# A hand-searched instruction order cut to the first half of weight conversion, and value-mean moves unchained, in a block-attention and gated-product kernel

## Chip, cores and metric

The kernel runs on one core of a Trainium2 chip. The metric is the device time of one execution in microseconds, as the median of several runs. PE is TensorE (matmuls), DVE is VectorE, ACT is ScalarE, POOL is GpSimd, and SP is SyncE, whose queue issues almost all transfers.

## The reference

```python
def attention(q, k, v):              # 4 sequences, 8 heads, 768 tokens, 64 wide
    k_sum = k.reshape(B, H, 24, 32, 64).max(axis=3)
    v_sum = v.reshape(B, H, 24, 32, 64).mean(axis=3)
    local = where(abs(pos_q - pos_k) < 16, q @ k.T / 8, -1e9)
    short = q @ k_sum.T / 8 + log(32)
    a = softmax(concat([local, short]))
    return a @ concat([v, v_sum])

def moe(x, w_a, w_b, w_out):         # x: 3072 x 512, hidden width 1536
    return ((x @ w_a) * (x @ w_b)) @ w_out
```

The output of the attention, with the heads laid side by side, is the x of the second part. All is float32.

## The kernel before

**Work and tiles.** The 3072 tokens are cut into tiles of 128, and these into ten chunks u = 0 to 9: three of two tiles for each of the first two sequences (u0 to u2, u3 to u5), two of three tiles for each of the last two. A chunk's attention makes scores (line 649), a softmax, transposed probabilities (line 786) and the product with the values (line 802). Its second part goes over twelve slices f = 0 to 11 of the hidden width. One *item* is a chunk and a slice: on PE the two products with w_a and w_b (line 1058, "hidden pair", 24 matmuls for chunks of two tiles), then ACT copies one (line 1090), DVE multiplies (line 1093), ACT rounds (line 1095), DVE subtracts to get the remainder (line 1098), and PE adds the product with w_out (line 1135, "down", 6 matmuls) one item later. Every operand is held as a high and a low half, so that one product takes three matmuls.

**Weights.** The 36 parts of the weights (a slice's a, b, o) are loaded by SP (line 373, tiles raw) and converted into the two halves by `convert(i)`: ACT (398) writes one word's value to a slot, DVE (401) writes a second word to a PSUM bank (c0 or c1), DVE (409) joins them, ACT (414) writes the high half, POOL (417) the low half. Parts from 18 on share the slots S0.0, S0.1, S1.0, S1.1. Chunks u0 and u1 run interleaved while this goes on. u2 (`FILL = 2`) is the "third attention": its score tiles use the banks c0 and c1, which the conversion uses too.

**The second sequence.** u3 opens it. `prep_keys(1)` loads its keys in four sets (tiles kin, and S for every other one), DVE transposes them (line 537) and takes block maxima. `prep_values(1)` loads the values, POOL sums them to block means in the tile vm, and eight moves on SP copy vm into the space S0 (`summed`), from which they are copied into the values' tiles vw. The room S0.2 and the keys in the list `PU` stand for the same space, used by the third attention. The values' tiles vw serve one score tile at a time: `bring(1)` loads them anew once the first tile's product has run.

**Order.** Every operation is given to `Work` with an engine, a rank, an assumed duration and the keys that it reads and writes; a write follows all earlier uses of its key. `emit` runs once, when the program is built, and writes the instructions out. Each engine keeps this order on the chip. For engines with a list in `ORDER`, the listed operations come exactly in that order:

```python
if fixed.get(e):
    return [o for o in ops if o.index == fixed[e][-1]]
return [o for o in ops if o.index not in listed]
```

When an engine's list is used up, the planner takes, of the operations that are ready by its assumed durations, the one with the lowest rank. Line numbers below are those of the kernel before; the changed kernel has them up to 13 lines earlier.

Of the kernel before, what the change touches and what calls it, by code (L numbers as in the profile page):

```python
# [21 lines left out]

ORDER = {
# [7 lines left out]
    ],  # L31
    "ACT": [
# [11 lines left out]
    ],  # L44
    "DVE": [
# [12 lines left out]
    ],  # L58
    "POOL": [
# [4 lines left out]
    ],  # L64
# [6 lines left out]
    ],  # L71
}

# [76 lines left out]
def attention_moe(  # L150
# [10 lines left out]
    nc = tc.nc  # L161
# [156 lines left out]
    work = Work({"POOL": 10.2, "DVE": 2.3, "ACT": 2.3, "PE": 3.0, "SP": 0.8})  # L318
# [4 lines left out]
    def act(rank, takes, reads, writes, fn):  # L323
        work.add("ACT", rank, takes, 0.16, reads, writes, fn)

    def dve(rank, takes, reads, writes, fn):
        work.add("DVE", rank, takes, 0.19, reads, writes, fn)
# [51 lines left out]
    def convert(i):  # L379

        rank = CONVERT + i / 12
        bk, (space, x) = f"c{i % 2}", ROOMS[i >= EARLY][i % len(ROOMS[i >= EARLY])]
        room = f"{space}.{x}"
        z = bank[bk].rearrange("p (m n) -> p m n", n=P)
        e = slot(space, x)[0].rearrange("p (m n) -> p m n", n=P)
        raw, hi, lo = f"raw{i}", f"hi{i}", f"lo{i}"

        def word(x):  # L390
            return raws[i].rearrange("p (m n t) -> p m n t", n=P, t=2)[:, :, :, x]

        def half(x):
            if i not in homes:
                homes[i] = wp.tile([P, 4, 2, P], F32R, tag=f"P{i}", name=f"w{i}")
            return homes[i][:, :, x, :]

        act(CHAIN, 0.57, [raw], [room], lambda: nc.scalar.activation(  # L398
            e, word(1).bitcast(F32), AF.Prelu, scale=2.0**-112, alpha=-(2.0**32)
        ))  # L400
        dve(rank, 0.6, [raw], [bk], lambda: nc.vector.tensor_scalar(
            out=z.bitcast(I32), in0=word(0).bitcast(U32), scalar1=2.0**-29, scalar2=7.0,
            op0=ALU.mult, op1=ALU.min,
        ))
        near = i in ON_DVE
        t, key = (z, bk) if near else (e, room)
        dve(
            rank, 0.6, [room, bk], [raw, key],
            lambda: nc.vector.scalar_tensor_tensor(
                out=t.bitcast(I32), in0=e.bitcast(I32), scalar=3, in1=z.bitcast(I32),  # L410
                op0=ALU.logical_shift_left, op1=ALU.bitwise_or,
            ),
        )
        act(rank - 0.5, 0.52, [key, raw], [hi], lambda: nc.scalar.copy(out=half(0), in_=t))  # L414
        (dve if near else pool)(
            rank, 0.6 if near else 1.24, [hi, key], [lo],
            lambda eng=nc.vector if near else nc.gpsimd: eng.tensor_tensor(  # L417
                out=half(1), in0=t, in1=half(0).bitcast(F32), op=ALU.subtract
            ),
        )  # L420
# [99 lines left out]
    def prep_keys(b):  # L520
        rank = LATER + 2 * b - 0.5
        if b == 1:
            work.add("-", 0, 0, 0, (), ["S1.2", "S1.3"], lambda: None)
        for c in range(NP):
            i = c % 2 if b == 1 else 0
            kw = kins[i]
# [37 lines left out]
    def prep_values(b):  # L564
# [7 lines left out]
        def add(n, out, i0, i1, writes):  # L572
# [2 lines left out]
                lambda: nc.gpsimd.tensor_tensor(out=out, in0=i0, in1=i1, op=ALU.add),  # L575
            )

        for hg in range(2):
            vv = v[b, 4 * hg : 4 * hg + 4].rearrange("h (n t) d -> (h n) t d", t=BLK)
            y, pk = vm[: 4 * NS, hg], f"vm{hg}"  # L580
            for i in range(BLK // T):
# [14 lines left out]
                        add(n, x[:, :n], x[:, :n], x[:, n : 2 * n], keys)  # L596
                        add(n, y, y, x[:, :n], keys + [pk])
            pool(
                rank, 0.3, (), [pk],
                lambda y=y: nc.gpsimd.tensor_scalar(  # L600
                    out=y, in0=y, scalar1=1.0 / BLK, scalar2=None, op0=ALU.mult
                ),
            )
            for h in range(4):
                load(
                    99, 6.0, 20, [pk], [VS[4 * hg + h]] + (["S0.2"] + PU if b == 1 else []),
                    summed(b)[:, 4 * hg + h], y[h * NS : (h + 1) * NS],
                )

# [14 lines left out]
    def scores(u, t, qT, qk, s, sk, banks, lead=None, way="AA"):  # L624
# [65 lines left out]
        for h in range(2):  # L690
# [18 lines left out]
            else:  # L709
                for c in range(NP):  # L710
                    more = {"accum_out": sums[:, c : c + 1]} if way[h] == "A" else {}
                    act(
                        rank, 0.44 if more else 0.32, [f"{mk}m{h}", xk[h]],
                        ([f"{mk}l{h}{c}"] if more else []) + ([ek[c]] if masked else []),
                        lambda h=h, c=c, more=more: nc.scalar.activation(  # L715
                            y[h][:, c, :], x[h][:, c, :], AF.Exp, bias=m[:, 0, h, c : c + 1],
                            scale=1.0, **more,
                        ),
                    )
            if way[h] != "A":  # L720
# [16 lines left out]
                lambda r=r, sums=sums: nc.vector.reciprocal(out=r, in_=sums),  # L737
            )
            pool(
                rank, 1.05, lk, ek if masked else [sk[h]],  # L740
                lambda h=h, r=r: nc.gpsimd.tensor_tensor(  # L741
                    out=y[h], in0=y[h], in1=r[:, :, None].broadcast_to([P, NP, COLS]),
                    op=ALU.mult,
# [102 lines left out]
    def first_attention():  # L846
# [31 lines left out]
        for n in range(4):  # L878
# [7 lines left out]
            )  # L886
            if MEANS[n] == "D":
                dve(
                    FIRST, 1.1, key, [f"vr{n}"],
                    lambda x=x, hg=hg, a=a: nc.vector.tensor_reduce(  # L890
                        out=rows[:, hg, a, :], in_=x.rearrange("p (t d) -> p d t", d=D),
                        axis=AX.X, op=ALU.add,
# [2 lines left out]
            else:  # L895
                m = 512
# [355 lines left out]
```

## Time and profile before

| what | value |
| --- | --- |
| median of three runs | 683.91 us (683.86 to 684.71) |
| profiled execution, its own time | 683.99 us |
| its span in the trace | 682.2 us, 13881 instructions |
| PE busy | 648.0 us (95%) |
| DVE busy | 403.5 us (59%) |
| ACT busy | 247.8 us (36%) |
| POOL busy | 156.1 us (23%) |

The busy times are sums over the whole span, and the engines are busy at different times: POOL, DVE and ACT do most of the conversion in the first 120 us, PE alone carries the rest. A share of the span therefore says little on one stretch; the rows further down are read by stretch.

### The profile page before, as it was taken

What the parts mean: (1) busy time and instruction counts of PE and PEld (TensorE: products, weight loads), DVE (VectorE), ACT (ScalarE), POOL (GpSimd) and SP (SyncE); (2) the same over time, 40 slices, a digit from 0 to 9 for tenths busy, and PEclk for the clock granted to TensorE, in tenths of its full rate; (3) what the DMA queues carried; (4) which work ended last, traced back from release to release, by engine and by line L of the source; (5) the groups of instructions that cost most, each with busy time, mean ns of one, the idle gap of its engine ahead of it and who ended that gap; (6) DMA issues with size and microseconds to landing.
All of it is one profiled execution on the core that took longest, in us unless ns stands there. A gap on an engine that the chain in (4) does not pass through costs nothing.

```text
span 682.2 us, 13881 instructions
## 1 busy us (share of the span) xinstructions
PE 648.0 (95%) x5384; PEld 607.4 (89%) x5384; DVE 403.5 (59%) x905; ACT 247.8 (36%) x748; POOL 156.1 (23%) x236
## 2 busy tenths in 40 slices
PE   5699999999955999999999999999999999999997
PEld 4488999899945999999999999999999999999996
DVE  4887779655566776945767777476767451121112
ACT  4798576321332333313433431243333421121111
POOL 6686264312533334301111010011111100000000
PEclk9699999999985999999999999999999999999999
DMA  9999950086235223432311213132211200010001
GB/s 210 261 310 235 313 176 1 2 163 142 71 93 102 61 62 65 106 56 52 76 38 38 68 38 60 33 84 39 40 24 25 69 1 1 1 46 1 1 1 46
DMA packets 153897, 54.76 MB, mean 80 GB/s; under 512 B 133976, under 2 KB 146520, under 8 KB 153832
## 3 DMA queue, kind: packets, MB, share of 16 engines
q1 hardware_dynamic: 153688, 53.75, 33.2%
q8 instruction: 42, 0.69, 0.4%
q14 instruction: 23, 0.19, 0.1%
q10 hardware_dynamic: 144, 0.13, 0.1%
HBM read 47.12 MB, written 6.29 MB: 78 GB/s over the span
## 4 chain that ended last, share of the span: by engine, by line
PE 85%; SPq 7%; DMA 3%; DVE 3%; ACT 1%; issue 1%; POOL 0%
PE h L1058 53%; PE o L1135 26%; SPq L335 6%; PE o L802 3%; PE c L649 3%; DMA raw<-in_moe_w_a_dram 2%; SPq L373 1%; DMA space<-in_v_dram 1%; DVE pt L786 1%; PE c L802 0%; DMA vw<-S 0%; DVE qT L1010 0%; PE c L1058 0%; DMA S<-vm 0%; ACT S L398 0%
## 5 line engine op out<-in xcount | busy, mean ns | idle before, releaser
L1058 PE MATMUL h<-x,w 128*128 128x256 f32 (+1 forms) x2488 | 397.8, 296 | 1.1 <-ACT x L821 0.7
L1058 PEld LDWEIGHTS h<-x,w 128*128 128x128 f32 x2488 | 356.9, 192 | 6.1 <-ACT x L821 0.9
L1058 PE MATMUL h<-late,w 128*128 128x256 f32 (+1 forms) x380 | 115.3, 303 | 0.1
L1135 PE MATMUL o<-w,gh 128*128 128x512 f32 x426 | 107.3, 383 | 0.0
L786 DVE STREAM_TRANSPOSE pt<-s 32x256 f32<-32x256 f32 x228 | 99.3, 436 | 11.7 <-POOL s L741 7.6
L741 POOL TENSOR_TENSOR s<-s,nml 128x480 f32<-128x480 f32 x44 | 43.4, 987 | 221.1 <-DVE nml L737 190.6
L1121 DVE TENSOR_TENSOR h<-h,g 128x384 f32<-128x384 f32 x47 | 26.6, 567 | 106.5 <-PE h L1058 106.3
L1135 PEld LDWEIGHTS o<-w,gh 128*128 128x128 f32 x426 | 76.3, 189 | 9.7 <-issue 1.4
L715 ACT ACTIVATE s<-s,nml 128x120 f32<-128x120 f32 x160 | 61.3, 385 | 42.6 <-DVE nml L686 42.5
L1123 ACT CAST gh<-h 128x384 fp32r<-128x384 f32 x47 | 22.5, 478 | 149.0 <-DVE h L1121 146.2
L1058 PEld LDWEIGHTS h<-late,w 128*128 128x128 f32 x380 | 73.3, 193 | 1.5 <-DVE late L825 0.4
L1093 DVE TENSOR_TENSOR h<-h,g 128x256 f32<-128x256 f32 x72 | 31.0, 431 | 67.9 <-ACT g L1090 67.4
L1090 ACT COPY g<-h 128x256 f32<-128x256 f32 x72 | 26.9, 373 | 116.3 <-PE h L1058 116.3
L1135 PE MATMUL o<-w,gl 128*128 128x512 f32 x213 | 59.7, 380 | 0.0
L1135 PE MATMUL o<-w,x 128*128 128x512 f32 x225 | 55.4, 382 | 0.4 <-ACT x L1095 0.3
L1135 PEld LDWEIGHTS o<-w,x 128*128 128x128 f32 x225 | 40.5, 189 | 6.7 <-ACT x L1095 1.3
L1135 PEld LDWEIGHTS o<-w,gl 128*128 128x128 f32 x213 | 40.1, 189 | 5.8 <-issue 0.2
L575 POOL TENSOR_TENSOR S<-S 96x256 f32<-96x256 f32 (+3 forms) x58 | 33.0, 570 | 46.0 <-DMA S<-in_v_dram 43.1
L1118 ACT COPY g<-h 128x384 f32<-128x384 f32 x48 | 23.0, 479 | 40.6 <-PE h L1058 40.1
L417 POOL TENSOR_TENSOR w<-S,w 128x512 fp32r<-128x512 f32 x24 | 30.5, 1284 | 30.2 <-ACT w L414 21.4
L1126 DVE TENSOR_TENSOR gl<-h,gh 128x384 fp32r<-128x384 f32 x47 | 26.2, 556 | 17.3 <-ACT gh L1123 16.8
L678 DVE SCALAR_TENSOR_TENSOR s<-c,mask 128x480 f32<-128x480 f32 x40 | 26.0, 653 | 14.4 <-PE c L649 14.2
(132 smaller groups left out, 572.2 us busy)
## 6 DMA issues: line engine op xcount, KB each, us to landing
raw<-in_moe_w_out_dram SPq DMA_DIRECT2D x12, 512.0 KB
raw<-in_moe_w_a_dram SPq DMA_DIRECT2D x12, 512.0 KB
raw<-in_moe_w_b_dram SPq DMA_DIRECT2D x12, 512.0 KB
out_dram<-S SPq DMA_DIRECT2D x23, 256.0 KB
S<-in_v_dram SPq DMA_DIRECT2D x24, 192.0 KB
kin<-in_k_dram SPq DMA_DIRECT2D x38, 100.0 KB
vw<-in_v_dram SPq DMA_DIRECT2D x17, 192.0 KB
qin<-in_q_dram SPq DMA_DIRECT2D x192, 16.0 KB
```

Of the source, the lines that this page charges most:

```text
L335: lambda: nc.sync.dma_start(out=out, in_=in_), rate=rate,
L417: lambda eng=nc.vector if near else nc.gpsimd: eng.tensor_tensor(out=half(1), in0=t, in1=half(0).bitcast(F32), op=ALU.subtract),
L575: lambda: nc.gpsimd.tensor_tensor(out=out, in0=i0, in1=i1, op=ALU.add),
L715: lambda h=h, c=c, more=more: nc.scalar.activation(y[h][:, c, :], x[h][:, c, :], AF.Exp, bias=m[:, 0, h, c : c + 1], scale=1.0, **more,),
L741: lambda h=h, r=r: nc.gpsimd.tensor_tensor(out=y[h], in0=y[h], in1=r[:, :, None].broadcast_to([P, NP, COLS]), op=ALU.mult,),
L786: lambda js=js, qs=qs, rs=rs: nc.vector.transpose(out=pv[js, rs, qs], in_=sv[qs, rs, js]),
L1058: nc.tensor.matmul(ps, w[:, c, part, :], inputs_of(u, xpart)[:, :, c].rearrange("p g (a b) -> p g b a", a=2), start=(i == 0), stop=(i == n ...
L1090: act(CHAIN, 0.38, [hk], [gk], lambda: nc.scalar.copy(out=g, in_=pa))
L1093: lambda: nc.vector.tensor_tensor(out=pa, in0=pb, in1=g, op=ALU.mult),
L1121: lambda: nc.vector.tensor_tensor(out=pb, in0=pb, in1=g, op=ALU.mult),
L1126: lambda: nc.vector.tensor_tensor(out=gl, in0=pb, in1=gh.bitcast(F32), op=ALU.subtract),
L1135: nc.tensor.matmul(bank[ok[j]], (gh if first else gl)[:, j * P : (j + 1) * P], w[:, :, part, :].rearrange("p (z a) n -> p z n a", a=2), st ...
```

## The change

Three things are edited. The lists of `ORDER` are new and shorter: they end with the operations around the nineteenth part of the weights, where the old ones went on to the last part (PE's list has 58 entries, before 104). All that follows is left to the planner. Within the new lists, neighbours are swapped. Second, each move of a value mean of sequence 1 now *reads* the room S0.2 and no longer *writes* S0.2 and the `PU` keys; so the eight moves no longer follow one another in a fixed chain, and the marker operation of `prep_keys(1)` (engine "-", it emits nothing) writes S0.2 and `PU` once instead. Third, five assumed durations are other numbers; they only sway the planner. No instruction is added or removed.

```diff
 ORDER = {
     "PE": [
-        13, 9, 1, 21, 5, 74, 94, 17, 72, 92, 75, 95, 118, 120, 125, 53, 59, 127, 128, 145,
+        9, 1, 5, 21, 13, 17, 72, 74, 75, 92, 94, 95, 118, 120, 125, 145, 53, 59, 127, 128,
...
@@ def convert(i)
-        act(CHAIN, 0.57, [raw], [room], lambda: nc.scalar.activation(
+        act(CHAIN, 0.68, [raw], [room], lambda: nc.scalar.activation(
-        dve(rank, 0.6, [raw], [bk], lambda: nc.vector.tensor_scalar(
+        dve(rank, 0.66, [raw], [bk], lambda: nc.vector.tensor_scalar(
@@ def prep_keys(b)
-            work.add("-", 0, 0, 0, (), ["S1.2", "S1.3"], lambda: None)
+            work.add("-", 0, 0, 0, (), ["S1.2", "S1.3", "S0.2", *PU], lambda: None)
@@ def prep_values(b)
+        room = ["S0.2"] if b == 1 else []
-                rank, 0.3, (), [pk],
+                rank, 0.37, (), [pk],
-                    99, 6.0, 20, [pk], [VS[4 * hg + h]] + (["S0.2"] + PU if b == 1 else []),
+                    99, 6.0, 20, [pk] + room, [VS[4 * hg + h]],
                     summed(b)[:, 4 * hg + h], y[h * NS : (h + 1) * NS],
...
```

The other three changed durations are those of an exponential (0.44 to 0.42), of the normalising product on POOL (1.05 to 0.95) and of a value mean on DVE (1.1 to 1.8).

**PE, at the first scores of u3.** In these rows h0 and h1 are the banks of hidden pairs, o0 and o1 those of downs, c0 and c1 those of scores; w with its number is a part of the weights. Before, the scores stand behind the hidden pair of u2's slice 9:

```order
L1058 MATMUL h0_75<-x_134,w24_1260 128x256 x12
L1058 MATMUL h0_75<-x_134,w25_1305 128x256 x12
L1135 MATMUL o0_71<-w23_1227,x_134 128x512 x2
L1135 MATMUL o1_72<-w23_1227,x_134 128x512 x2
L1058 MATMUL h1_76<-x_134,w27_1322 128x256 x12
L1058 MATMUL h1_76<-x_134,w28_1369 128x256 x12
L649 MATMUL c0_77<-kT_79,qT_142 64x120 x2
L649 MATMUL c1_78<-kT_79,qT_142 64x120 x2
```

With the change, the same place is:

```order
L1046 MATMUL h0_75<-x_134,w6_599 128x256 x12
L1046 MATMUL h0_75<-x_134,w7_630 128x256 x12
L1123 MATMUL o0_71<-w5_634,x_134 128x512 x2
L1123 MATMUL o1_72<-w5_634,x_134 128x512 x2
L1046 MATMUL h1_76<-x_134,w9_693 128x256 x12
L1046 MATMUL h1_76<-x_134,w10_706 128x256 x12
L637 MATMUL c0_77<-kT_79,qT_142 64x120 x2
L637 MATMUL c1_78<-kT_79,qT_142 64x120 x2
```

Parts 27 and 28 are slice 9, parts 9 and 10 slice 3: the first scores of u3 stand six items of u2 earlier.

**DVE, at the end of the conversion.** The tile qT holds the transposed queries of u2's second tile, raw33 to raw35 are the last three parts, and h, g, gh, gl and x belong to items. Before:

```order
L401 TENSOR_SCALAR c0_77<-raw34_922 128x512
L1093 TENSOR_TENSOR h0_75<-h0_75,g_135 128x256
L786 STREAM_TRANSPOSE pt_128<-s_127 32x8x32
L409 SCALAR_TENSOR_TENSOR S1_146<-S1_146,c0_77 128x512
L401 TENSOR_SCALAR c1_78<-raw35_1022 128x512
L1098 TENSOR_TENSOR gl_137<-h0_75,gh_136 128x256
L1010 STREAM_TRANSPOSE qT_142<-qin_141 128x512
L786 STREAM_TRANSPOSE pt_128<-s_127 32x8x32
L409 SCALAR_TENSOR_TENSOR S1_146<-S1_146,c1_78 128x512
```

With the change:

```order
L388 TENSOR_SCALAR c1_78<-raw33_1035 128x512
L396 SCALAR_TENSOR_TENSOR S0_147<-S0_147,c1_78 128x512
L388 TENSOR_SCALAR c0_77<-raw34_972 128x512
L1081 TENSOR_TENSOR h1_76<-h1_76,g_135 128x256
L396 SCALAR_TENSOR_TENSOR S1_146<-S1_146,c0_77 128x512
L388 TENSOR_SCALAR c1_78<-raw35_1018 128x512
L1086 TENSOR_TENSOR x_134<-h1_76,x_134 128x256
L396 SCALAR_TENSOR_TENSOR S1_146<-S1_146,c1_78 128x512
L998 STREAM_TRANSPOSE qT_142<-qin_141 128x512
L674 TENSOR_REDUCE nml0_143<-s_127 128x4 x2
```

The transposed probabilities of u2's first tile (L786, pt) no longer stand between the conversions: the softmax of that tile now goes on behind the last part, and the second tile's queries follow the conversion at once.

**SP, from the store of u0 to the copies of the second sequence's value means.** out_dram is a store, S_147<-vm a move of a value mean, vw<-S the copy of means into the values' tiles. Before, at the last loads of keys and the moves:

```order
L335 DMA S_146<-in_k_dram 32x25x32 x4
L335 DMA S_146<-in_v_dram 96x512 x2
L335 DMA S_147<-vm 24x64 x4
L335 DMA kin<-in_k_dram 32x25x32 x4
L335 DMA S_146<-in_v_dram 96x512 x4
L335 DMA qin<-in_q_dram 32x8x32 x16
L335 DMA S_147<-vm 24x64
L335 DMA S_146<-in_v_dram 96x512
L335 DMA S_147<-vm 24x64 x3
L335 DMA out_dram<-S_146 128x512 x2
L335 DMA vw_129<-S_147 24x512
L335 DMA vw_130<-S_147 24x512
```

With the change:

```order
L322 DMA out_dram<-S_147 128x512 x2
L322 DMA S_146<-in_k_dram 32x25x32
L322 DMA S_146<-in_v_dram 96x512 x2
L322 DMA S_146<-in_k_dram 32x25x32 x3
L322 DMA vw_129<-in_v_dram 80x8x64
L322 DMA vw_130<-in_v_dram 32x8x64
L322 DMA vw_130<-in_v_dram 64x8x64
L322 DMA S_147<-vm 24x64 x7
L322 DMA S_146<-in_k_dram 32x25x32 x4
L322 DMA S_147<-vm 24x64
L322 DMA kin<-in_k_dram 32x25x32 x2
```

Seven moves now stand together, and the two sets of keys that go through S stand on both sides of them, behind the store of u0's output.

## Rows read from the trace of the kernel before

**Rows 1.** Page, part 2: PE's busy tenths in 40 slices of the span.
```profile
PE   5699999999955999999999999999999999999997
```

**Rows 2.** Table of windows; the first row names the columns.
```profile
core 0: us, PE busy (x) PEld busy (x) DVE busy (x) ACT busy (x) POOL busy (x), PEclk, DMA share, GB/s
28.00:57.00 29.00, 26.71 (x310) 23.45 (x308) 23.76 (x49) 26.77 (x73) 24.50 (x25) 0.97 1.02 266
60.20:195.70 135.50, 135.11 (x1152) 126.88 (x1152) 88.07 (x200) 61.58 (x160) 51.43 (x60) 1.00 0.50 127
76.00:94.40 18.40, 18.40 (x143) 17.76 (x144) 12.91 (x25) 11.70 (x28) 7.11 (x7) 1.00 1.03 334
94.40:120.00 25.60, 25.60 (x196) 24.20 (x198) 22.95 (x46) 17.96 (x40) 14.49 (x12) 1.00 0.01 2
195.70:216.00 20.30, 6.03 (x97) 5.17 (x97) 15.95 (x36) 4.80 (x20) 7.38 (x14) 0.62 0.43 103
```

**Rows 3.** Timeline of PE: start, length, work, [idle before and what ended it].
```profile
60.13 5.62 PE L1058 MATMUL h<-x,w 128*128 128x256 f32 x48
...
119.83 1.05 PE L649 MATMUL c<-kT,qT 64*64 64x120 f32 x32
...
182.26 1.05 PE L649 MATMUL c<-kT,qT 64*64 64x120 f32 x32
...
194.02 1.67 PE L1135 MATMUL o<-w,x 128*128 128x512 f32 x6
203.05 1.88 PE L649 MATMUL c<-kT,qT 64*64 64x120 f32 x32 [7.36 <-DVE nml L731]
...
224.13 1.03 PE L1135 MATMUL o<-w,gh 128*128 128x512 f32 x4
```

**Rows 4.** Chain that ended last: start, length, what.
```profile
171.70 2.68 PE h L1058 x24
...
178.35 1.30 PE o L1135 x6
...
182.33 0.99 PE c L649 x32
...
232.24 1.08 PE o L802 x32
```

**Rows 5.** Waits of the DMA queue on SP: total, times, longest.
```profile
SPq L335 <- PE c L802: 48.7, 1, 48.7
```

**Rows 6.** Timeline of SP's issues.
```profile
86.45 0.52 SPq L373 DMA_DIRECT2D raw<-in_moe_w_a_dram  x1
135.78 2.23 SPq L335 DMA_DIRECT2D vw<-in_v_dram  x3
...
161.42 2.38 SPq L335 DMA_DIRECT2D S<-in_k_dram  x4
...
165.82 3.27 SPq L335 DMA_DIRECT2D S<-vm  x4
```

**Rows 7.** Timeline of DVE.
```profile
76.09 0.66 DVE L678 SCALAR_TENSOR_TENSOR s<-c,mask 128x480 f32<-128x480 f32 x1 [0.47 <-PE c L649]
...
92.52 0.43 DVE L1093 TENSOR_TENSOR h<-h,g 128x256 f32<-128x256 f32 x1 [2.70 <-ACT g L1090]
...
116.31 0.69 DVE L409 SCALAR_TENSOR_TENSOR S<-S,c 128x512 int32<-128x512 int32 x1
116.91 0.74 DVE L401 TENSOR_SCALAR c<-raw 128x512 int32<-128x512 uint32 x1
117.57 0.41 DVE L1098 TENSOR_TENSOR gl<-h,gh 128x256 fp32r<-128x256 f32 x1
117.90 0.70 DVE L1010 STREAM_TRANSPOSE qT<-qin 128x512 f32<-128x512 f32 x1
...
172.18 0.77 DVE L537 STREAM_TRANSPOSE kT<-S 128x576 f32<-128x576 f32 x1
...
193.13 0.43 DVE L1093 TENSOR_TENSOR h<-h,g 128x256 f32<-128x256 f32 x1 [2.22 <-ACT g L1090]
...
197.05 2.69 DVE L786 STREAM_TRANSPOSE pt<-s 32x256 f32<-32x256 f32 x6
```

More of the change, by code (lines that the diff above doesn't have):

```diff
@@ L712, in scores @@
                     act(
-                        rank, 0.44 if more else 0.32, [f"{mk}m{h}", xk[h]],
+                        rank, 0.42 if more else 0.32, [f"{mk}m{h}", xk[h]],
                         ([f"{mk}l{h}{c}"] if more else []) + ([ek[c]] if masked else []),
@@ L739, in scores @@
             pool(
-                rank, 1.05, lk, ek if masked else [sk[h]],
+                rank, 0.95, lk, ek if masked else [sk[h]],
                 lambda h=h, r=r: nc.gpsimd.tensor_tensor(
@@ L888, in first_attention @@
                 dve(
-                    FIRST, 1.1, key, [f"vr{n}"],
+                    FIRST, 1.8, key, [f"vr{n}"],
                     lambda x=x, hg=hg, a=a: nc.vector.tensor_reduce(
```

61 rows, old and new, of the table ORDER are left out of this document.

## The prediction

> **What bounds the kernel now.** I read the page's slices first: PE, which does the matmuls, is near full after the first two slices except in slices 12 and 13 [rows 1]. The table of windows puts numbers on that: from 60.2 to 195.7 us PE is busy 135.11 of 135.50 us, so nothing can be won there; from 195.7 to 216.0 it is busy 6.03 of 20.30 us, and its granted clock means 0.62 [rows 2]. So before the change there is one hole, and it is read from both edges. In PE's timeline the work ahead of it ends at 194.02 + 1.67 = 195.69 us, and the first down product of chunk u3 comes at 224.13 [rows 3]. Between them stand one score tile, two value tiles and the two hidden pairs ahead of that down product. The chain gives their sizes at the full clock: hidden pair (H) 2.68, down (D) 1.30, scores (S) 0.99, values (V) 1.08 us [rows 4]. That is 0.99 + 2 x 1.08 + 2 x 2.68 = 8.51 us of work in 28.44 us: **19.9 us lost**. Idle time is 20.30 - 6.03 = 14.3 of it; the other 5.6 us are work at the lower clock (1.2 GHz), which was granted while PE stood with gaps.
>
> Why is there a hole? Chunk u3 opens the second sequence. Its first score tile runs only at 182.26 and PE has little filling work left for the softmax that follows [rows 3]. The queue that loads its keys tells why it is late: SP issued its last weight load at 86.45, then stood 48.7 us on the values product of u2's first tile, whose buffers the next load takes, and issued again at 135.78 [rows 5, 6]. In PE's order that product stands behind u2's second score tile (119.83, [rows 3]), and that one waits for the end of the weight conversion on DVE.
>
> **What the order does.** The same instructions exist in both programs, so I count PE's units in the printed orders from one common start, the first H of u0's slice 4 at 60.13 [rows 3], and check the method on the old one:
> - u2's second scores: before 15 H, 14 D, 1 S ahead: 60.13 + 40.2 + 18.2 + 1.0 = 119.5 (trace 119.83). After: 11 H, 9 D, 1 S: 102.3.
> - values of u2's first tile, on which SP stood: before 18 H, 18 D, 2 S: 133.8 (SP moved on at 135.78). After 14 H, 12 2/3 D, 2 S: 116.1.
> - u3's first scores: before 30 H, 28 D, 2 S, 2 V: 181.1 (trace 182.26, 1.2 more). After 24 H, 22 D, 2 S, 2 V: 157.2 + 1.2 = 158.4.
>
> So u3's scores are issued 24 us earlier, behind slice 3 of u2 and not slice 9, and both values products of u3 find hidden pairs and downs of u2 ahead of them. The units in front of u3's first H remain the same work (the count gives 196.8 in the old order, 195.5 in the new). If everything arrives in time, PE goes from 60 us through 224 us without a hole: **-19.9 us**.
>
> **What this costs.**
> *Conversion.* The second scores of u2 need DVE's transposed queries, which now stand behind all conversions. Between u2's first scores (DVE at 76.09) and that transpose the new order has 16 conversions, 14 multiply or subtract instructions of items, 2 score copies and the transpose. By start-to-start times in [rows 7], a conversion is 0.66 + 0.60 = 1.26, an item's instruction 0.33, a copy 0.66, the transpose 0.70 us: 20.2 + 4.6 + 1.3 + 0.7 = 26.8 us. Without a gap it ends at 102.9. DVE has gaps: while weights still arrived it was busy 12.91 of 18.40 us (70%), and afterwards 22.95 of 25.60 us (90%) [rows 2]. At 90% the end is 76.1 + 29.8 = 105.9, which is 3.6 us behind 102.3; with 0.2 of drift in the count, **+3.4 us**. At 70% it is 114.4, +11.9 us; with no gap, +0.4. I take 90% because the late stretch is where conversions stood close in the old trace, as they do in the new order.
>
> The rule that speaks against this: the Trainium skill, "TensorE: Matmul & The Clock Gate", the table at its head, says that the queues of ScalarE, VectorE and GpSimd are strictly first in, first out, and only TensorE pulls weight loads ahead. By that rule each item's multiply that DVE meets early blocks the conversions behind it. The trace agrees: DVE stood 2.70 us at 92.52 on such a multiply [rows 7]. By that reading the sum would be that of rival B.
>
> *Softmax of u3's first tile.* Its values product stands 14.8 us behind the start of its scores (2 S, 3 H, 2 D and the first 0.87 of a third). In the old trace the transposed probabilities were complete at 197.05 + 2.69 = 199.74, 17.5 us after 182.26; 2.22 us of that was DVE waiting at the head of its queue for an item [rows 3, 7]. The new order has five transposes ahead of the next item, so I take 17.5 - 2.2 = 15.3: **+0.5 us** (bounds 0 and 2.7).
>
> *Start.* The first 36 instructions on POOL are the same set in both orders, and POOL is busy 24.50 of 29 us there [rows 2]. ACT and DVE only swap neighbours: 0, with 1.5 us either way, a third of POOL's 4.5 us of slack.
>
> *Moves of value means.* No longer chained through a written room, seven of the eight are issued one behind the other. Each costs SP 0.82 us (four in 3.27, [rows 6]) and moves 6 KB; the chain itself emits nothing. Their cover is that values of u3 come 14.8 us after its scores. The changed cost figures of the planner emit nothing either.
>
> **Sum.** 683.99 (the profiled execution's own time, 0.08 above the median of the runs) - 19.9 + 3.4 + 0.5 = **668.0 us**.
>
> **Rivals.**
> - **A, as above**: 664 to 671 us, 0.66.
> - **B, the conversion's tail slips.** DVE keeps the 70% share because items block its queue: stall 11.9, so 676.5 us, and PE idles once near 102 to 114. For it: the wait of 2.70 us in [rows 7]. Against: the 90% of [rows 2]. 0.14.
> - **C, the keys are late behind u0's store.** In SP's new order two of four key sets stand behind the store of u0. The last D of u0 has 17 H, 15 D, 2 S, 1 V ahead of its end: 128.3, and with four instructions of 0.7 us to copy out, 131. Then six issues at 0.6 us (four took 2.38, [rows 6]) and the next set: a set took 10.8 us from issue (161.42) to its transposes (172.18) and at most 10.1 to the scores at 182.26 [rows 3, 6, 7]. Both late sets use one buffer, so at worst 131 + 3.6 + 10.8 + 10.8 + 10.1 = 166.3 against 158.4: up to 7.9 us, with half of it 672 us. If the seven moves also hold SP (5.7 us), 678. 0.12.
> - **D, the other side.** The path from SP's release to u3's scores keeps its old length, 182.26 - 135.78 = 46.5 us [rows 3, 6]. From 131 the scores then run at 177.5, PE idles 19.1 us in the middle of u2 with nothing to fill it, and comes back at the lower clock (5.6 us as before): 668.0 + 24.7 = 692.7 us. It is slower than before once the path exceeds 40 us (683.99 + 1.4 - 668.0 - 5.6 = 11.8 us of stall, scores at 170.2). Against: two key sets are issued ahead of the store, and SP is released for these 17.7 us sooner than before (116.1 against 133.8). 0.05.
> - **E, no effect.** u3's inputs come only when they did before, the hole merely stands elsewhere: 684 us, 0.03.
>
> **How the numbers follow.** 0.2% (1.4 us) is about what a measurement here tells from no change. A, B and C (0.92) are faster, D (0.05) is slower, and E falls within the bound but for 0.01: 0.93, 0.02, 0.05. The range goes from A's low end (no stall at all: 683.99 - 19.9) to just above B, 664.0 to 677.0; left out are D, E and C's worst.
>
> **What will show it.** Right: PE's slices near full from the third on, no wait of PE above 4 us between 60 and 230 us, u2's second scores at 103 to 107 and u3's first at 158 to 163 us; SP's long stand much shorter than 48.7 us; granted clock 1.00 through 200 to 224 us. Step by step: conversions ended on DVE near 106; the keys' last transposes before 158; probabilities of u3's first tile within 16 us of its scores. Wrong: a PE wait above 8 us on the transposed queries (B), a wait on keys near 160 us (C, D), or a hole of the old size at another place. The prediction would also fail if the start, in which everything is listed anew, lost more than 1.5 us ahead of 60 us.

## The result and the profile after

The changed kernel takes 666.21 us (665.67 to 666.73, four runs), the kernel before 684.19 us in the same comparison: ratio 0.9736, interval 0.9720 to 0.9753. The forecast was 668.0 us (664.0 to 677.0). The profiled execution took 666.73 us, with a span of 664.6 us. Two executions among all the runs stand far off the rest and count in no comparison: one of the kernel before at 856 us, and the profiled one of the cut-only kernel below at 1709 us, so that no rows of that kernel are read.

The page's PE slices and, below, the windows that answer to [rows 1] and [rows 2]; 77.38 to 105.11 us is the end of the conversion on DVE:

```profile
PE   5789999999999999999999999999999999999997
```

```profile
core 0: us, PE busy (x) PEld busy (x) DVE busy (x) ACT busy (x) POOL busy (x), PEclk, DMA share, GB/s
60.20:195.70 135.50, 133.77 (x1226) 125.46 (x1223) 105.37 (x235) 67.19 (x187) 60.75 (x78) 1.00 0.56 144
195.70:216.00 20.30, 20.30 (x205) 19.13 (x203) 14.02 (x34) 8.31 (x34) 8.95 (x17) 1.00 0.37 98
77.38:105.11 27.73, 26.47 (x204) 25.34 (x202) 27.12 (x49) 23.57 (x44) 20.70 (x17) 1.00 0.78 229
```

Slices 12 and 13 are full. Between 195.7 and 216.0 us PE was busy 6.03 us before and is busy 20.30 us now, at the full granted clock (1.00, before 0.62). Nothing else of that size changed. PE's waits between 60 and 230 us are two, and the timeline shows where they and the main products stand; it answers to [rows 3]:

```profile
PE c L637 <- DVE qT L998: 1.3, 1, 1.3
PE o L1123 <- POOL w L404: 0.4, 1, 0.4
```

```profile
60.53 5.62 PE L1046 MATMUL h<-x,w 128*128 128x256 f32 x48
...
74.72 1.35 PE L1123 MATMUL o<-w,x 128*128 128x512 f32 x5 [0.39 <-POOL w L404]
...
105.17 1.05 PE L637 MATMUL c<-kT,qT 64*64 64x120 f32 x32 [1.31 <-DVE qT L998]
...
119.22 1.15 PE L790 MATMUL c<-pt,vw 120*64 120x64 f32 x32
...
160.72 1.05 PE L637 MATMUL c<-kT,qT 64*64 64x120 f32 x32
...
175.86 1.15 PE L790 MATMUL o<-pt,vw 120*64 120x64 f32 x32
```

u2's second scores run at 105.17 (before 119.83), its first values at 119.22, u3's first scores at 160.72 (before 182.26). SP's timeline answers to [rows 6]:

```profile
83.17 1.47 SPq L360 DMA_DIRECT2D raw<-in_moe_w_a_dram  x1
84.69 6.52 SPq L322 DMA_DIRECT2D vw<-in_v_dram  x3
91.25 5.89 SPq L322 DMA_DIRECT2D kin<-in_k_dram  x4
105.14 0.81 SPq L322 DMA_DIRECT2D qin<-in_q_dram  x2
...
109.74 2.46 SPq L322 DMA_DIRECT2D kin<-in_k_dram  x4
...
120.29 2.13 SPq L322 DMA_DIRECT2D vw<-in_v_dram  x3
...
134.07 1.39 SPq L322 DMA_DIRECT2D out_dram<-S  x2
...
142.10 5.60 SPq L322 DMA_DIRECT2D S<-vm  x7
147.80 3.45 SPq L322 DMA_DIRECT2D S<-in_k_dram  x4
```

SP's waits, which answer to [rows 5], have 2.1 us where 48.7 us stood:

```profile
SPq L322 <- PE c L790: 2.1, 1, 2.1
```

This list differs from the one before in two ways, and the prediction's account of the hole spoke of only one. The load of the second tile's values (vw at 120.29) is released 15.5 us sooner than at 135.78. And it no longer stands at the head: before, it came right behind the weights, and everything for u3 behind it; now two of u3's four key sets are issued ahead of it, at 91.25 and 109.74. (Under rival D the prediction noted two key sets ahead of u0's store, but not that they pass the blocked load.) Which of the two filled the hole is what the experiments ask.

### The profile page after: what moved, and what is told of

Same layout as the page of the kernel before. It is cut to its first block, busy times and chain, and to the rows that moved or that the text cites. A ratio compares the mean times of both kernels' runs of the same rounds, so it can differ in the third digit from the quotient of the medians.

```text
span 664.6 us, 13879 instructions
## 1 busy us (share of the span) xinstructions
PE 644.6 (97%) x5384; PEld 604.2 (91%) x5384; DVE 405.8 (61%) x905; ACT 247.6 (37%) x748; POOL 156.4 (24%) x236
## 4 chain that ended last, share of the span: by engine, by line
PE 83%; SPq 6%; DMA 6%; DVE 3%; issue 1%; ACT 0%; ACTq 0%
PE h L1046 51%; PE o L1123 26%; SPq L322 4%; DMA raw<-in_moe_w_a_dram 3%; PE o L790 3%; PE c L637 3%; SPq L360 2%; DMA raw<-in_moe_w_b_dram 2%; DVE S L396 1%; DVE c L388 1%; DMA raw<-in_moe_w_out_dram 1%; PE c L790 0%; PE c L1046 0%; DVE h L1081 0%; ACT S L385 0%
## 5 line engine op out<-in xcount | busy, mean ns | idle before, releaser
L774 DVE STREAM_TRANSPOSE pt<-s 32x256 f32<-32x256 f32 x228 | 99.3, 436 | 10.8 <-POOL s L729 6.7
L1078 ACT COPY g<-h 128x256 f32<-128x256 f32 x72 | 26.8, 373 | 115.1 <-PE h L1046 115.1
L666 DVE SCALAR_TENSOR_TENSOR s<-c,mask 128x480 f32<-128x480 f32 x40 | 26.0, 652 | 14.3 <-PE c L637 14.0
```

The source lines that it names most:

```text
L774: lambda js=js, qs=qs, rs=rs: nc.vector.transpose(out=pv[js, rs, qs], in_=sv[qs, rs, js]),
L1078: act(CHAIN, 0.38, [hk], [gk], lambda: nc.scalar.copy(out=g, in_=pa))
```

## The experiments

**Which edit carries the gain?** Four kernels take the change apart.

*The cut alone.* The old lists, in their old order, end where the new ones end; PE's:

```diff
-        326, 533, 534, 542, 549, 556, 547, 548, 554, 555, 561, 562, 570, 563, 575, 576, 584,
...
+        326, 533, 534, 542,
```

> The kernel before with one edit: its own lists, in their old order, end where the new ones end; moves still chained, old planner costs. Theory (the cut alone lets the planner put the conversion in one piece, u2's second scores early and u3's scores early): u2's second scores run near 103 to 107 us, the hole at 196 to 216 us is gone, time 664 to 671 us. By count u3's first scores now stand at 137 us, so a wait of PE for the keys near 137 to 150 us is possible, up to 10 us, and would be the upper end. Rival (the moves' chain or the searched start made the gain): a hole of 10 us or more remains and the time is above 678 us.

Measured 669.04 us (667.93 to 669.35, three runs), ratio 0.9782 (0.9764 to 0.9800). The cut carries most of the gain: 15 of 18 us.

*The moves alone.*

```diff
-            work.add("-", 0, 0, 0, (), ["S1.2", "S1.3"], lambda: None)
+            work.add("-", 0, 0, 0, (), ["S1.2", "S1.3", "S0.2", *PU], lambda: None)
...
+        room = ["S0.2"] if b == 1 else []
...
-                    99, 6.0, 20, [pk], [VS[4 * hg + h]] + (["S0.2"] + PU if b == 1 else []),
+                    99, 6.0, 20, [pk] + room, [VS[4 * hg + h]],
```

> The kernel before with one edit: the moves read the room and the marker writes it, as in the change; full old lists. Theory: PE's order is word for word that of before, u2's second scores stay at 120 us, SP stands 48 us as before, and the hole stays: 682 to 686 us, no difference above 0.3%. Rival (the chain of the moves kept the keys and means late): the hole shrinks by the time of the copies of the means, 3 to 15 us, time 669 to 681 us.

683.94 us, ratio 1.0001 (0.9987 to 1.0015): nothing, as the theory had it. The waits are those of before to a tenth.

*All but the moves.* The reverse of that diff on the changed kernel.

> The changed kernel with the moves chained again and the old marker. By the orders all four key sets now stand ahead of u0's store and u3's first scores six units earlier, near 138 us. Theory: u3's inputs are early either way, so 664 to 671 us; a wait of PE for keys near 138 us of 0 to 5 us is what could differ. Rival (the unchained moves carry part of the gain): slower than the changed kernel by 3 us or more, with waits on means or probabilities between 160 and 216 us.

667.58 us, ratio 0.9770 (0.9752 to 0.9788). No wait for keys came: u3's scores run at 139.43. But the values products behind them wait, in PE's timeline:

```profile
103.52 1.05 PE L636 MATMUL c<-kT,qT 64*64 64x120 f32 x32 [1.53 <-DVE qT L997]
162.45 0.34 PE L789 MATMUL o<-pt,vw 120*64 120x64 f32 x4 [0.73 <-DMA vw<-S]
163.56 1.04 PE L789 MATMUL o<-pt,vw 120*64 120x64 f32 x28 [0.78 <-DVE nml L724]
174.22 1.04 PE L789 MATMUL o<-pt,vw 120*64 120x64 f32 x28 [0.23 <-DVE pt L773]
```

These three waits are 1.7 us that the changed kernel does not have. The kernel's interval overlaps with that of the changed one, so this pair alone does not prove it; the last experiment does.

*The start alone.* The first half in the new order, the second half listed as before.

```diff
-        13, 9, 1, 21, 5, 74, 94, 17, 72, 92, 75, 95, 118, 120, 125, 53, 59, 127, 128, 145,
...
+        9, 1, 5, 21, 13, 17, 72, 74, 75, 92, 94, 95, 118, 120, 125, 145, 53, 59,
...
```

> The kernel before with only the first half of its lists put into the new order; the second half listed as before, old chain and costs. Theory: the searched start is worth within 1.5 us either way and the hole stays: 682.5 to 686 us. Rival (the start carries the gain): below 678 us, with the first hidden pair of slice 4 well ahead of 60.1 us.

684.35 us, ratio 1.0008 (0.9999 to 1.0018), with the old hole still there. The newly searched start is worth nothing that shows in the total.

**Are the late second scores the cause?** In the changed kernel PE's list goes on with its old second half; DVE, ACT, POOL and SP stay cut.

```diff
-        326, 533, 534, 542,
+        326, 533, 534, 542, 549, 556, 547, 548, 554, 555, 561, 562, 570, 563, 575, 576, 584, 568,
...
```

> The changed kernel, but PE's list goes on with the old second half, so u2's second scores stand behind 15 hidden pairs again (near 120 us) and its first values near 134; DVE, ACT, POOL and SP stay cut. DVE's conversion stays in one piece and ends near 105. Theory (SP's release by u2's first values product decides when u3's keys come): SP stands on that product until 134 to 136 us, u3's keys are complete near 168 to 172 us, PE waits 3 to 8 us on them at the count's 165 us; time 669 to 676 us. Rival 1 (the conversion in one piece is what matters): 665 to 668 us. Rival 2 (the late scores alone bring the whole hole back): 680 to 686 us.

666.85 us, ratio 0.9748 (0.9728 to 0.9769). The forecast from the theory, 669 to 676, failed, though its first two events came as named: PE's timeline has the second scores and the first values as late as before the change. The wait for keys did not come: u3's scores run at 167.04, and PE is busy 19.95 of 20.30 us between 195.7 and 216.0. The number is that of Rival 1 (the conversion in one piece is what matters); whether its reason holds, the last pair of kernels below decides.

```profile
120.85 1.05 PE L638 MATMUL c<-kT,qT 64*64 64x120 f32 x32
...
135.28 1.15 PE L791 MATMUL c<-pt,vw 120*64 120x64 f32 x32
...
167.04 1.05 PE L638 MATMUL c<-kT,qT 64*64 64x120 f32 x32
```

From SP's release to u3's scores it is now 167.04 - 136.35 = 30.7 us, where the kernel before took 46.5. The same run's SP timeline shows why: two key sets are out before the values' load is released.

```profile
89.87 5.38 SPq L323 DMA_DIRECT2D kin<-in_k_dram  x4
...
125.34 2.04 SPq L323 DMA_DIRECT2D kin<-in_k_dram  x4
...
136.35 2.39 SPq L323 DMA_DIRECT2D vw<-in_v_dram  x3
```

So a second theory: not how long SP stands, but what stands behind it. SP's old list ended with the three loads of those values (634, 635, 633). As long as a listed operation is outstanding, `emit` lets nothing unlisted onto that engine; all of u3's loads are unlisted. This is the planner at work, before anything runs on the chip.

*The scores 8 us later, and one down later.* PE's list goes on with the planner's own order, with entry 454 (u2's second scores) moved back.

```diff
-        326, 533, 534, 542,
+        326, 533, 534, 542, 549, 547, 548, 556, 554, 555, 563, 561, 562, 570, 568, 569, 577, 575,
+        576, 584, 582, 583, 589, 590, 591, 598, 454,
```

For one down later, the list has 454 right behind 583.

> The changed kernel with PE listed a little further, so that u2's second scores stand two downs and two hidden pairs (8 us) later, near 112 us; the rest is planned. Theory: the wait of 1.3 us on the transposed queries goes; the first values follow 8 us later, but u3's keys had 2.4 us to spare and the planner sets u3's scores 2 to 4 us later too, so 0 to 4 us of new waits near 165 us: 665 to 670 us. Rival (every us that the second scores are late shows in the time): 672 to 675 us.

666.76 us, ratio 0.9758 (0.9727 to 0.9789), and no wait for u3's keys; the rival's 672 to 675 is out. The second scores ran at 112.47, but the first values did not follow 8 us later, as expected: they ran at 118.92 (119.22 in the changed kernel). So SP was released no later, and this run says nothing on a late release.

> The changed kernel with u2's second scores one down (1.3 us) later in PE's list, just where the transposed queries are ready. Theory: the wait of 1.31 us there goes and nothing else moves: 664.5 to 665.5 us. Rival (the work is only moved, since the keys or the probabilities of u3 follow later): 666 to 668 us.

666.46 us, ratio 0.9744 (0.9726 to 0.9761): no gain. The wait on the queries fell from 1.31 to 0.20 us, but downs beside it now wait 1.0 us for ACT's rounded product. The wait was only moved, as the rival had it, though to downs of u2 and not to u3's inputs.

*The old durations.*

> The changed kernel with the five assumed durations of before. They emit nothing; the planner sets u2's first values one hidden pair later and all eight moves behind u0's store. Theory: within 1 us of the changed kernel, 665 to 668 us, since PE is full either way. Rival (the durations keep PE's plan close to what the chip does, and carry the rest of the gain over the cut alone): 668 to 672 us.

666.62 us, ratio 0.9753 (0.9735 to 0.9771): no measurable part of the gain.

**Three entries.** The kernel before, with one line edited:

```diff
-        405, 411, 322, 417, 435, 429, 447, 423, 399, 634, 635, 633,
+        405, 411, 322, 417, 435, 429, 447, 423, 399,
```

> The kernel before with one edit: the last three entries of SP's old list (the loads of the values for u2's second tile, which wait for u2's first values product) are no longer listed; all other lists stay whole, the moves chained, the old durations. By the order two key sets and one set of values now stand ahead of those loads, and u3's first scores behind 26 hidden pairs, 165 us by count. New theory (what stands on SP behind the blocked loads made u3 late, not how long they are blocked): u2's second scores still at 120 us and its first values at 134, yet the hole at 196 to 216 us is gone or under 5 us: 665 to 672 us. Theory on record (late second scores and values make u3 late): 680 to 686 us.

666.53 us, ratio 0.9757 (0.9738 to 0.9775). This is the whole gain, to the measurement, from three numbers. The window of the hole is nearly full, with PE busy 19.77 of 20.30 us:

```profile
195.70:216.00 20.30, 19.77 (x200) 18.19 (x203) 15.26 (x37) 7.89 (x29) 7.32 (x14) 1.00 0.35 89
```

PE's timeline again has the second scores at 119.61 and the first values at 134.37, as before, and u3's scores 15.8 us earlier, four items of u2 sooner in PE's order:

```profile
119.61 1.05 PE L649 MATMUL c<-kT,qT 64*64 64x120 f32 x32
...
134.37 1.15 PE L802 MATMUL c<-pt,vw 120*64 120x64 f32 x32
...
166.47 1.05 PE L649 MATMUL c<-kT,qT 64*64 64x120 f32 x32
```

SP's timeline between the last weights and the release, which in the kernel before is empty [rows 6]:

```profile
86.70 0.51 SPq L373 DMA_DIRECT2D raw<-in_moe_w_a_dram  x1
87.26 8.80 SPq L335 DMA_DIRECT2D S<-in_k_dram  x4
96.10 2.25 SPq L335 DMA_DIRECT2D kin<-in_k_dram  x4
118.40 0.31 SPq L335 DMA_DIRECT2D qin<-in_q_dram  x1
...
135.45 1.67 SPq L335 DMA_DIRECT2D vw<-in_v_dram  x2
```

PE waits for u3's keys neither here nor in the kernel before: its order is written when the program is built, and the planner puts u3's scores where, by its assumed durations, the keys will be ready. The plan alone does not make the difference, though. In the kernel before, POOL's timeline has the last copy of block maxima, after which the keys are complete, 4.4 us ahead of the scores at 182.26:

```profile
177.51 0.31 POOL L469 COPY kT<-ksum 128x144 f32<-128x144 f32 x1 [1.70 <-DVE ksum L558]
```

Without keys arriving sooner, u3's scores could thus have come at most 4.4 us earlier.

**And back.** Two kernels put the three loads back, behind the weights (SP's list whole), one with PE's old second half and one with PE cut. The other three entries, 322 to 324, are the loads for u2's first tile; the changed kernel issues them at that same place without a list (vw at 84.69 above), so listing them moves nothing.

```diff
-        417, 441, 447, 411, 423, 435,
+        417, 441, 447, 411, 423, 435, 323, 324, 322, 634, 635, 633,
```

> The kernel of the late-scores run (PE's list goes on with its old second half) with SP's list whole too, so that the three loads stand right behind the weights and all of u3's keys behind them. New theory: SP stands 45 to 50 us until 136, u3's scores at 181 to 184 us, the hole of 17 to 21 us is back, although DVE's conversion stays in one piece and the moves are free: 682 to 687 us. Rival (the conversion in one piece was enough in that run): 665 to 670 us.

685.43 us, ratio 1.0026 (1.0015 to 1.0037). The hole is back, with DVE's conversion in one piece, the moves free and the new start all in place, so the conversion in one piece was not what mattered in the run with PE's old second half. Nor was it what held the second scores: here DVE had their queries ready at 104.81 (a transpose of 0.70 us from 104.11), and PE, by its list, came to them at 121.65. The windows and PE's timeline:

```profile
195.70:216.00 20.30, 6.71 (x92) 5.33 (x93) 16.41 (x37) 4.30 (x18) 7.34 (x14) 0.73 0.44 105
```

```profile
183.71 1.05 PE L638 MATMUL c<-kT,qT 64*64 64x120 f32 x32
...
204.50 1.88 PE L638 MATMUL c<-kT,qT 64*64 64x120 f32 x32 [7.36 <-DVE nml L720]
...
212.28 0.48 PE L791 MATMUL o<-pt,vw 120*64 120x64 f32 x4 [4.00 <-DVE pt L775]
215.00 1.76 PE L791 MATMUL o<-pt,vw 120*64 120x64 f32 x28 [2.24 <-DVE pt L775]
```

> The changed kernel with only SP's list whole (the three loads right behind the weights); PE plans its scores early, so u2's first values run near 119 us and SP is released near 121. New theory: all of u3's keys then follow that release by the old path of some 46 us, ready near 167 us against scores at 161 by count: a wait of 2 to 8 us, 668 to 675 us. Rival (any order of SP does once u2's values are early): 665 to 667.5 us.

668.65 us, ratio 0.9784 (0.9766 to 0.9803). Here SP issues the last three of six value loads at 118.98, with all of u3 behind them, and the path from there to u3's scores (163.21) is 44.2 us, nearly the old 46.5. It fits because it starts 16.8 us sooner (118.98 against 135.78). SP's timeline, then PE's:

```profile
83.40 37.56 SPq L321 DMA_DIRECT2D vw<-in_v_dram  x6
121.05 0.95 SPq L321 DMA_DIRECT2D S<-in_v_dram  x2
```

```profile
163.21 1.05 PE L636 MATMUL c<-kT,qT 64*64 64x120 f32 x32
...
183.65 0.34 PE L789 MATMUL o<-pt,vw 120*64 120x64 f32 x4 [2.12 <-DVE s L665]
```

Beside the wait for the transposed queries, which the changed kernel has too, what is left are waits of 2.12 us on DVE and 0.61 us on the means at u3's first values product (183.65 us), not on the keys.

So there are two levers, what SP has listed and when PE runs u2's second scores, and each alone fills the hole:

| | SP's three loads listed | not listed |
| --- | --- | --- |
| PE's old second half (second scores near 121) | 685.43 | 666.85 |
| PE planned (second scores near 104 to 105) | 668.65 | 666.21 |

**What the moves are worth beside the cut.** The cut-only kernel with the moves unchained.

> The cut-only kernel with the moves unchained as in the change: old lists in their old order, cut, old durations. u3's first scores go from 137 back to about 161 us by count, behind slice 3 or 4 of u2. If the moves' chain is what the cut alone paid over the changed kernel (planned too early, u3's products wait for the copies of the means): 665.5 to 667 us, as the changed kernel. If the searched start or the durations make the difference: 668 to 670 us, as with the cut alone.

665.55 us, ratio 0.9739 (0.9725 to 0.9754), against 0.9764 to 0.9800 for the cut alone: the intervals do not touch. With the lists cut, unchaining is worth about 3 us beside the old start (beside the new one, the pair above has 1.4 us between the medians, not clear of noise); without the cut it is worth nothing. What the chain costs beside the cut is shown only by the waits of that pair. It is as fast as the changed kernel, without the new start and the new durations, so those add nothing that was measured. No kernel of these is measurably faster than the changed one.

## Why the prediction was right, and where its reason was not

**The hole, -19.9 us: right in size.** Idle time of 14.3 us and the low clock are both gone in the window 195.7 to 216.0.

**The cause of the hole: half right.** The prediction said that u3 was late because SP stood 48.7 us on u2's first values, and that this product was late for the conversion's sake. The stand was real and an earlier release is enough (668.65 against 685.43 us). In the kernel of 685.43 us, though, the conversion ended early and the product stayed late: PE's list alone held it. And the earlier release is not needed: with the release at 135.45 as before, freeing three loads on SP gives the same time. The step that failed is the reading of [rows 5, 6]: it took the length of the wait for the cause and did not ask which transfers behind it needed it at all. The keys did not; only their place in the list made them wait. The forecast of the time did not hang on this step: the places of the units were counted in the printed orders, which hold both levers. Rival D's premise, that the path keeps its 46.5 us, fails for the same reason. D counted it from u0's store; from there (134.07) to u3's scores (160.72) it was 26.7 us, since two key sets were out before.

**The conversion, +3.4 us: mis-sized.** PE waited 1.31 us. The stretch began 1.3 us later than counted (77.38, not 76.09), which PE did as well: it stood ready at 103.86, not 102.5. The transpose ended at 105.11, so the stretch took 27.7 us where 26.8 was counted without gaps and 29.8 with the share of 90%. DVE was busy 27.12 of 27.73 us, 98%. Rival B's price came from a stretch in which DVE stood idle for 5.5 us [rows 2]. DVE's waits in that stretch of the kernel before put 5.3 us of it down to items that DVE met before ACT had done its part:

```profile
DVE h L1093 <- ACT g L1090: 3.9, 3, 2.7
DVE x L1098 <- ACT x L1095: 1.4, 1, 1.4
```

In the new order DVE stood idle for 0.6 us in the whole 27.7. The Trainium skill's rule of strict queues ("TensorE: Matmul & The Clock Gate", table at its head) does not speak against the new order: DVE's heads were ready nearly all the time, as the 0.6 us show, and a ready head holds nothing up.

**The softmax, +0.5 us: right within its bounds.** u3's first values follow its scores by 175.86 - 160.72 = 15.1 us, with no wait. (The 14.8 us of the prediction are the sum with three downs and part of a fourth, as the trace has them; its list names only two and part of a third.) The transposes of probabilities end at 175.64 in DVE's timeline, 0.2 us ahead:

```profile
173.40 2.24 DVE L774 STREAM_TRANSPOSE pt<-s 32x256 f32<-32x256 f32 x5
```

**The start, 0 with 1.5 either way: right.** Slice 4 begins at 60.53 against 60.13, +0.4; the run of the start alone gives the same time as before.

**Rival C did not come, by little.** u0's store left at 134.07 (131 was counted), seven moves took 5.60 us (5.7), and the last key set followed at 147.80. It took 5.9 us to its transposes, not 10.8:

```profile
153.68 0.77 DVE L524 STREAM_TRANSPOSE kT<-S 128x576 f32<-128x576 f32 x1
```

The last copy of block maxima on POOL ended at 158.34, 2.4 us before the scores.

**The moves: costed at nothing, right only for the edit alone.** Together with the cut and the old start, the chain costs about 3 us; with the new start, 1.4 us between the medians.

**The sum.** -19.9 (hole) + 1.3 (queries) + 0.4 (low half of a weight at 74.72) + 0.4 (start) = -17.8 us, against 666.73 - 683.99 = -17.3 us between the two profiled executions. The 0.5 us left are within the spread of the runs (665.67 to 666.73). Against the same execution the forecast was 1.3 us too high (1.8 against the median): the conversion was 2.1 and the softmax 0.5 too high, the two terms of 0.4 were put at nothing, and the 0.5 us left has the other sign. The errors partly cancel.

## What to carry to other kernels

SP issued nothing between 86.97 and 135.78 us, since its queue went by its order. Where a queue does so, look past the instruction that waits to those behind it: what mattered here was less the 48.7 us of waiting than which work stood there without needing the wait. With a planner like this one, a list that fixes an order should end before its first entry with a long wait, since the planner can only put other work behind such an entry, never ahead. And when a change moves much at once, undo its parts in pairs: either of two levers was enough here, so undoing one alone showed little (666.85 and 668.65 against 666.21 us) and hid the cause.

## What was not expected of the hardware

With its inputs nearly always ready, DVE was 98% busy over 27.7 us of mixed conversion and item instructions, where the kernel before, in another order, had 70% and 90% in its two stretches [rows 2]. A share read in one order was thus no limit for the next.
